# A third end slot of at most 32 rows, worked inside the last 256-row slot of a mixture-of-experts kernel

## The chip, the cores and the metric

The kernel runs on one core of a Trainium2 chip. The metric is the device time of one execution in microseconds, lower is better. Besides the times there is one profiled execution of the kernel before, whose trace is read below.

## The reference

A soft-capped attention feeds a layer of experts, of which every token goes to one:

```python
def _attn_ref(q, k, v, cap):                     # q, k, v: 8 x 12 x 448 x 64
    scores = cap * np.tanh(np.matmul(q, k.transpose(0, 1, 3, 2)) / np.sqrt(64) / cap)
    attn = softmax(scores)
    return np.matmul(attn, v)
...
x = attn_out.transpose(0, 2, 1, 3).reshape(3584, 768)
logits = x @ w_gate + modality_bias[modality_id]         # 8 experts
e_idx = np.argmax(logits, axis=1)
gate_w = softmax(logits)[np.arange(N), e_idx]
for e in range(8):
    mask = e_idx == e
    h = np.maximum(x[mask] @ w1[e], 0.0)                 # 768 x 1024
    out[mask] = gate_w[mask, None] * (h @ w2[e])         # 1024 x 768
```

With the reference's inputs the eight experts get 0, 245, 0, 1551, 0, 0, 0 and 1788 tokens.

## The kernel before, in words

**Attention and routing.** The first third of the run is attention in float32, in 64x64 tiles of TensorE. Each batch's rows of x are stored to DRAM, and a map is scattered there that has, region by region (one region for each expert), the token number, the gate weight and the softmax reciprocals of each row. `sums2` (L555) is the only place with 32-column tiles: four float32 products of 448 columns, each into its own 32 partitions of one PSUM bank, and four more behind them.

**Slots.** The experts' rows are worked in slots. A full slot has 384 rows (W, three tiles of 128). `slots` (L345) counts each expert's rows, gives it full slots as long as more than 256 rows are left, and sorts the remainders by size behind the full slots. Eight slots (one early one and seven, FIXED) are always run. What comes then depends on the data, and `slots` computes which of three endings fits: ENDS (L72) names their tiles, (2, 2, 1), (3, 2) and (3, 2, 1). `finish` (L1101) writes the endings as nested tests of one register. Only the body of the innermost one, ENDS[0], stands directly behind the tests:

```python
with tc.If(which == end + 1, preferred_fallthrough_block=end == 0) as branch:
```

ENDS[0] is three slots of 256, 256 and 128 rows; they are called A, B and C here.

**A slot** (`run_slot`, L1048). `gather` (L866) fetches the rows of the next slot from DRAM by an indirect DMA of POOL's queue. The weights of one expert are 6 raw blocks of W1 (512 KB each) and 8 of W2 (384 KB each). They are loaded on SP's queue into four staging buffers (`load_raw`, L888), and each is split into a rounded part (ScalarE, L899) and a remainder (VectorE, L900), so that three fast products take the place of one float32 product. `ffn1` (L934) makes 8 blocks of 128 hidden units, each over 6 blocks of the model dimension: for a slot of fewer than three tiles, two matmuls for each pair (L960, L961). Behind each block ScalarE and VectorE add the two halves (L968, L969), apply the rectifier (L972) and form the remainder (L973); in between stand the steps in `inside`: the last four W2 splits and the scaling of the next slot's rows (`norm`, L877). `ffn2` (L1000) makes, for each tile of 128 rows, two halves of 384 output columns, each from 24 matmuls (L1014), and between these halves the transposes of the next slot's rows (L916). ScalarE scales each half by the gate weight (L1030; the last half of all is cut between ScalarE and VectorE), and POOL scatters the tile to the output (L1043).

**Order of the work.** Engines take their instructions in order. An instruction that is pinned stays behind the one that was written before it on its engine; the others may be moved by the scheduler. SP's loads are pinned, and each waits for its staging buffer.

Of the kernel before, what the change touches and what calls it, by code (L numbers as in the profile page):

```python
# [52 lines left out]
NT, DM, FF, E, NM = B * S, H * D, 1024, 8, 2  # L53
# [7 lines left out]
TW = W // 128  # L61
RB = -(-NT // W)
RG = RB * W
NOROW = E * RG
ENTRY = 16
RECS = 4
HB = 32
# [1 line left out]
KC, FC = DM // 128, FF // 128  # L69
HALF = DM // 2  # L70
FIXED = 7
ENDS = ((2, 2, 1), (3, 2), (3, 2, 1))  # L72
MAXS = RB + E - 1
W2_EARLY = 4
LEAD = 3
# [10 lines left out]
class Program:  # L86
# [23 lines left out]
    def constants(self, cpool, dram):  # L110
        nc = self.nc
# [57 lines left out]
        self.blke = table("blke", [128, E, RB + 1], [[1, E], [0, RB + 1]])  # L169
        self.exp = table("exp", [128, E], [[1, E]])  # L170
        self.slot = table("slot", [128, 1], [[0, 1]], channel=1)

        self.acc = cpool.tile([CP, E], BF16, name="acc")
        nc.gpsimd.memset(self.acc, 0.0)
# [170 lines left out]
    def slots(self, pool, ps, early, then=None):  # L345
# [78 lines left out]
        if early:  # L424
            pair = tile("pair", [128, E])
            V.scalar_tensor_tensor(pair, rem, 128.0, sm, op0=ALU.is_gt, op1=ALU.mult)
            two = tile("two", [128, 1])
            V.tensor_reduce(two, pair, axis=AX.X, op=ALU.add)
            V.tensor_scalar(two, two, NB, float(FIXED + 2), op0=ALU.add, op1=ALU.is_le)
            first = tile("first1", [128, 1])  # L430
            V.scalar_tensor_tensor(first, NB, float(FIXED), two, op0=ALU.is_le, op1=ALU.mult)
            other = tile("other", [128, 1])
            V.scalar_tensor_tensor(other, NB, float(FIXED + 1), two, op0=ALU.is_le, op1=ALU.mult)
            V.tensor_tensor(other, other, first, op=ALU.subtract)
            V.tensor_scalar(begin, total, float(FIXED + 2), 2.0, op0=ALU.is_gt, op1=ALU.add)
            V.tensor_tensor(begin, begin, other, op=ALU.mult)
            V.tensor_tensor(end, begin, first, op=ALU.add)
            V.scalar_tensor_tensor(begin, first, 3.0, begin, op0=ALU.mult, op1=ALU.add)

            fits = tile("fits", [128, 1])  # L440
# [389 lines left out]
    def moe_pools2(self, st):  # L830
        pool = lambda name, bufs, **kw: st.enter_context(self.tc.tile_pool(name=name, bufs=bufs, **kw))
        wp = pool("wp2", 1)
        self.h = [wp.tile([128, FC, W], F32R, name=f"h{h}") for h in "hl"]
        self.w2s = [[wp.tile([128, DM], F32R, name=f"b{h}{k}") for h in "hl"] for k in range(W2_EARLY)]
        self.ps_h, self.ps_t, self.ps_y = (
            pool("ps_h", 3, space=PSUM), pool("ps_t", 2, space=PSUM), pool("ps_y", 2, space=PSUM)
        )
# [159 lines left out]
            finish(ph, f)  # L997
            hook("f", f)

    def ffn2(self, mt, n, between=(), wait=0, then=None, last=False):  # L1000

        nc = self.nc
        between = list(between)
        for t in range(n):
# [19 lines left out]
            for half in range(2):  # L1024
# [20 lines left out]
                bounds_check=NT - 1, oob_is_err=False,  # L1045
            )

    def run_slot(self, cur, n, ahead=None, raws=(), hooks=None, rows=None):  # L1048

# [23 lines left out]
        self.ffn2(cur[1], n, between=moves, wait=3 if hooks else 0, then=then if hooks else None, last=n < TW and not nxt)  # L1073
        return nxt

    def run_slots(self, cur, hooks):
# [24 lines left out]
    def finish(self, which, end, cur, ahead, rows):  # L1101

        tc = self.tc
        if end < 0:
            self.tail()
            return
        with tc.If(which == end + 1, preferred_fallthrough_block=end == 0) as branch:  # L1107
            at, self.last_sp = cur, None
            tiles = ENDS[end]
            for i, n in enumerate(tiles):  # L1110
                at = self.run_slot(
                    at, n, *((
                        lambda: ahead(FIXED + i + 1, tiles[i + 1]), (), None, lambda: rows(FIXED + i + 1, tiles[i + 1])
                    ) if i + 1 < len(tiles) else ())
                )
        with branch.Else():
            self.finish(which, end - 1, cur, ahead, rows)

# [119 lines left out]
    def build(self):  # L1238
        tc, nc = self.tc, self.nc
        with ExitStack() as st:  # L1240
# [3 lines left out]
            self.plani = self.cpool.tile([1, 3], I32, name="plani")  # L1244
            with ExitStack() as sa:
                qk = sa.enter_context(tc.tile_pool(name="qk", bufs=2))
                firsts = [qk.tile([128, FF], F32, name="kq") for _ in range(2)]
# [89 lines left out]
```

## Time and profile before

| | |
|---|---|
| median of 3 runs | 821.35 us (821.28 to 821.41) |
| the profiled execution, its own time | 819.97 us |
| its span, first to last instruction | 818.4 us |
| TensorE busy | 803.1 us, 98% of the span |
| VectorE, ScalarE, GpSimd busy | 518.5, 516.0, 139.2 us |
| moved by DMA | 148.44 MB, 181 GB/s over the span |

The busy time of an engine is the time in which it executed at least one instruction. Matmuls overlap, so a full TensorE row says that it had no gaps, not that it was at its peak. The time of one run lies some 1.6 us above the span of its profile, the median of the unprofiled runs 1.4 us above that run.

### The profile page before, as it was taken

To read this page: it belongs to the slowest core of one execution; us is meant where nothing else is said; L and a number is where in the kernel's file an instruction comes from. 1 tells how busy PE (TensorE), PEld (TensorE's weight loads), DVE (VectorE), ACT (ScalarE), POOL (GpSimd) and SP (SyncE) were. 2 spreads that over 40 slices of the span, in tenths; PEclk is the share of its full clock that TensorE was granted. 3 is DMA by queue.
4 is the path that set the end of the run, shared out by engine and by line. 5 is a ranking of instruction groups with operands and counts; after the bars stand their busy time and mean duration, and the time that the engine had idled before them with its cause. 6 is when DMAs were issued, how large, how long until landed. Compare 5 with 4: busy or idle time off the path is not lost. (4 is left out here: it accounts for less than half of the span.)

```text
span 818.4 us, 15444 instructions
## 1 busy us (share of the span) xinstructions
PE 803.1 (98%) x5988; PEld 608.9 (74%) x5988; DVE 518.5 (63%) x865; ACT 516.0 (63%) x655; POOL 139.2 (17%) x163
## 2 busy tenths in 40 slices
PE   7999999999999999999999999999999999999997
PEld 2333333333333348999999999999999999989996
DVE  4778888888788898764446344453544635447662
ACT  6999999999999994443444334444254443546562
POOL 2000220012021221451203113031120310111010
PEclk9999999999999999999999999999999999999999
DMA  5375536264454653977556365563665545557670
GB/s 187 116 218 194 144 131 203 74 200 147 149 181 137 189 188 89 274 233 277 208 178 230 117 216 209 189 204 135 205 230 186 200 151 183 167 190 254 219 222 29
DMA packets 57011, 148.44 MB, mean 181 GB/s; under 512 B 7758, under 2 KB 22366, under 8 KB 56928
## 3 DMA queue, kind: packets, MB, share of 16 engines
q1 hardware_dynamic: 48224, 113.34, 43.6%
q0 software_dynamic: 8560, 34.02, 11.6%
q8 instruction: 49, 0.80, 0.4%
q14 instruction: 34, 0.28, 0.1%
q10 hardware_dynamic: 144, 0.00, 0.0%
HBM read 114.44 MB, written 24.64 MB: 170 GB/s over the span
## 5 line engine op out<-in xcount | busy, mean ns | idle before, releaser
L961 PE MATMUL ph<-x,al 128*128 128x384 f32 (+2 forms) x510 | 159.9, 314 | 0.0
L1014 PE MATMUL py<-bh,hh 128*128 128x384 f32 x464 | 158.5, 342 | 0.4 <-ACT hh L972 0.3
L1014 PE MATMUL py<-bl,hh 128*128 128x384 f32 x464 | 155.6, 335 | 0.0
L1014 PE MATMUL py<-bh,hl 128*128 128x384 f32 x464 | 155.4, 335 | 0.0
L522 PE MATMUL xT<-pt,va 64*64 64x448 f32 x1344 | 151.8, 537 | 1.1 <-DVE xT L529 1.1
L494 ACT ACTIVATE pt<-sc 128x896 f32<-128x896 f32 x164 | 142.9, 906 | 11.4 <-PE sc L489 11.4
L497 ACT ACTIVATE pt<-pt 128x1792 f32<-128x1792 f32 x84 | 142.7, 1699 | 2.7
L510 DVE TENSOR_TENSOR tot<-tot,pt 128x896 f32<-128x896 f32 x118 | 127.7, 1082 | 10.8 <-ACT pt L497 6.4
L957 PE MATMUL ph<-x,ah 128*128 128x384 f32 x366 | 122.4, 334 | 0.0
L958 PE MATMUL ph<-x,ah 128*128 128x384 f32 x366 | 122.3, 334 | 0.0
L900 DVE TENSOR_TENSOR bl<-raw,bh 128x768 fp32r<-128x768 f32 x88 | 81.3, 954 | 52.6 <-ACT bh L899 52.6
L522 PEld LDWEIGHTS xT<-pt,va 64*64 64x64 f32 x1344 | 50.5, 133 | 73.7 <-issue 68.4
L1030 ACT ACTIVATE ot<-py,mt 128x384 f32<-128x384 f32 (+1 forms) x58 | 33.5, 579 | 102.6 <-PE py L1014 66.1
L972 ACT ACTIVATE hh<-ph 128x384 fp32r<-128x384 f32 x64 | 31.2, 491 | 105.7 <-PE ph L961 98.9
L961 PEld LDWEIGHTS ph<-x,al 128*128 128x128 f32 x510 | 96.0, 188 | 0.0
L900 DVE TENSOR_TENSOR al<-raw,ah 128x1024 fp32r<-128x1024 f32 x60 | 71.0, 1222 | 27.8 <-ACT ah L899 27.8
L1014 PEld LDWEIGHTS py<-bh,hh 128*128 128x128 f32 x464 | 87.1, 188 | 1.2 <-ACT hh L972 0.6
L1014 PEld LDWEIGHTS py<-bl,hh 128*128 128x128 f32 x464 | 87.2, 188 | 0.2 <-DVE bl L900 0.2
L1014 PEld LDWEIGHTS py<-bh,hl 128*128 128x128 f32 x464 | 87.1, 188 | 0.0
L899 ACT CAST bh<-raw 128x768 fp32r<-128x768 f32 x88 | 70.1, 836 | 24.2 <-DMA raw<-in_w_dram 24.0
L489 PE MATMUL sc<-kq 64*64 64x448 f32 x672 | 79.4, 547 | 3.7 <-ACT pt L494 2.6
L489 PE MATMUL sc<-kx 64*64 64x448 f32 x672 | 78.6, 540 | 0.8 <-ACT pt L494 0.8
(188 smaller groups left out, 909.6 us busy)
## 6 DMA issues: line engine op xcount, KB each, us to landing
raw<-in_w_dram SPq DMA_DIRECT2D x88, 384.0 KB, 4.5
raw<-in_w_dram SPq DMA_DIRECT2D x62, 512.0 KB, 4.1
kq<-in_kq_dram SPq DMA_DIRECT2D x24, 448.0 KB, 3.6
va<-in_v_dram SPq DMA_DIRECT2D x24, 448.0 KB, 5.5
kx<-in_kq_dram SPq DMA_DIRECT2D x24, 448.0 KB, 4.3
xd<-xs SPq DMA_DIRECT2D x32, 336.0 KB, 6.4
xr<-xg POOLq DMA_DIRECT2D x24, 384.0 KB, 3.1
mapd<-spare SPq DMA_DIRECT2D x4, 480.0 KB, 6.2
```

Source lines behind the costliest of these rows:

```text
L489: pin(pe.matmul(sc[i * KB : (i + 1) * KB, j, :S], kq[rows, s * KB : (s + 1) * KB], kq[rows, S:QK], start=True, stop=True,))
L494: pin(nc.scalar.activation(weights(n), sc[:, :, :S], AF.Tanh, scale=self.isc if slow else self.iscr))
L497: pin(nc.scalar.activation(pt, pt, AF.Exp, scale=self.cabsr))
L510: pin(V.tensor_tensor(tots[d], pt_of(n - 1) if s == 1 else tots[d], pt_of(n), op=ALU.add))
L522: pin(pe.matmul(self.xT[j * D : (j + 1) * D, i, :S], vas[d][rows, o : o + D], pt[rows, j], start=s == 0, stop=s == STEPS - 1,))
L899: keep((cast.tensor_copy if cast else self.nc.scalar.copy)(hi, raw))
L900: keep((minus or self.nc.vector).tensor_tensor(lo, raw, hi, op=ALU.subtract))
L957: keep(nc.tensor.matmul(ph[:, :w], hi[:, fs], self.x[:, k, 0, :w], start=first, stop=False))
L958: keep(nc.tensor.matmul(ph[:, :w], hi[:, fs], self.x[:, k, 1, :w], start=False, stop=False))
L961: keep(nc.tensor.matmul(ph[:, :w], lo[:, fs], self.x[:, k, 0, :w], start=False, stop=last))
L1014: nc.tensor.matmul(pys[half][:, :HALF], self.h[a][:, f, rows], self.w2s[f][c][:, cs], start=f == i == 0, stop=f == FC - 1 and i == 2,)
L1030: put = nc.scalar.mul(ot[:, half * HALF :][:, :cut], pys[half][:, :cut], mt[:, t, 1:2])
```

## The change

A fourth ending, (2, 2), is added. It is taken when the conditions of (2, 2, 1) hold and no more than two remainders have over 32 rows. The third remainder, of at most 32 rows, then has no slot of its own: its rows are gathered and scaled as 32 partitions, turned by six transposes (`few_turn`), and multiplied with the raw float32 weights, that are not split. The turned rows are the stationary operand (128 x 32) and the weights stream past them: a product over 128 of the model dimension is cut into four column groups of 32 columns, which write four 32-partition strips of one PSUM bank. So W1 takes 6 x 4 products of 256 columns (`few_first`), two transposes turn the hidden units (`few_back`), and W2 takes 8 x 4 products of 192 columns (`few_second`). The steps stand between the halves of slot B's `ffn2`. The fourteen raw blocks go to buffers that are free by then: the two first tiles of attention, a new tile `spare`, parts of the gathered rows' tile, and the four staging buffers.

```diff
-ENDS = ((2, 2, 1), (3, 2), (3, 2, 1))
+ENDS = ((2, 2, 1), (3, 2), (3, 2, 1), (2, 2))
+FEW = len(ENDS)
+FT = 32
+FG = 128 // FT
+FH, FY = FF // FG, DM // FG
...
+        for g in range(FG):
+            nc.gpsimd.memset(self.part[g * FT : (g + 1) * FT], float(g))
...
+            V.scalar_tensor_tensor(some, rem, float(FT), sm, op0=ALU.is_gt, op1=ALU.mult)
+            V.tensor_reduce(few, some, axis=AX.X, op=ALU.add)
+            V.tensor_scalar(few, few, NB, float(FIXED + 2), op0=ALU.add, op1=ALU.is_le)
+            V.tensor_tensor(few, few, first, op=ALU.mult)
+            V.scalar_tensor_tensor(end, few, float(FEW - 1), end, op0=ALU.mult, op1=ALU.add)
...
+        self.spare = wp.tile([128, DM], F32, name="w2f")
...
+                if 2 * t + half < len(besides):
+                    besides[2 * t + half]()
...
+    def few_rows(self):
+        few["e"] = self.register(nc.sync, meta[row : row + 1, 0:1], E - 1)
+        r = self.register(nc.gpsimd, meta[row : row + 1, 1:2], NOROW)
+        for g in range(FG):
+            self.pin(nc.gpsimd.dma_start(mt[g * FT : (g + 1) * FT], self.mapd[ds(r, FT)]))
+    def few_gather(self):
...
+    def few_ready(self):
+        self.pin(nc.vector.tensor_tensor(x, x, rec, op=ALU.mult))
+        self.pin(nc.vector.tensor_copy(spot, mt.bitcast(I32)[:, 0:1]))
+        self.pin(nc.vector.tensor_scalar(where, spot, float(FG), self.part, op0=ALU.mult, op1=ALU.add))
+        few["w1"] = [self.load_raw(few["e"], self.w1, k, FF, self.firsts[k]) for k in range(2)]
+        few["w2"] = [self.load_raw(few["e"], self.w2, 0, DM, self.spare)]
+    def few_weights(self):
+        few["w1"] += [self.load_raw(few["e"], self.w1, k, FF) for k in range(2, KC)]
+    def few_weights2(self):
+        dst = [self.xg[:, 2], self.xg[:, 0], self.firsts[0], self.firsts[1]] + [None] * 3
+        few["w2"] += [self.load_raw(few["e"], self.w2, f, DM, dst[f - 1]) for f in range(1, FC)]
+    def few_turn(self):
+        for k in range(KC):
+            self.pin(nc.tensor.transpose(
+                bank[:, k * FT : (k + 1) * FT], self.xg[:FT, 0, k * 128 : (k + 1) * 128], self.ident[:FT, :FT]
+            ))
+        self.pin(nc.scalar.copy(self.few["x"], ...))
+    def few_first(self):
+        for k in range(KC):
+            for g in range(FG):
+                self.pin(nc.tensor.matmul(
+                    bank[g * FT : (g + 1) * FT, :FH], few["x"][:, k], few["w1"][k][:, g * FH : (g + 1) * FH],
+                    start=k == 0, stop=k == KC - 1,
+                ))
+        self.pin(nc.scalar.activation(few["h"], bank[:, :FH], AF.Relu))
+        self.few_weights2()
+    def few_back(self):
+        for c in range(FH // 128):
+            self.pin(nc.tensor.transpose(bank[:, cs], few["h"][:, cs], self.ident))
+        self.pin(nc.scalar.copy(few["ht"], ...))
+    def few_second(self):
+        for f in range(FC):
+            for q in range(FG):
+                self.pin(nc.tensor.matmul(
+                    bank[q * FT : (q + 1) * FT, :FY], few["ht"][:, c, g * FT : (g + 1) * FT],
+                    few["w2"][f][:, q * FY : (q + 1) * FY], start=f == 0, stop=f == FC - 1,
+                ))
+        self.pin(nc.scalar.mul(ot[:, :FY], bank[:, :FY], few["mt"][:, 1:2]))
+        nc.gpsimd.indirect_dma_start(
...
     def run_slot(...):
+        if few:
+            inside += [self.few_ready, self.few_weights]
         self.ffn1(n, hooks, inside)
+        if few:
+            self.few_turn()
...
+                  besides=[self.few_first, self.few_back, self.few_second] if few else ())
...
     def finish(...):
+            tiles, few = ENDS[end], end + 1 == FEW
+            if few:
+                self.few_rows()
...
+                    at = self.run_slot(at, n, rows=self.few_gather if few else None, few=few)
```

## Rows read from the trace of the kernel before

**Rows 1.** Stretches: busy us of PE, PEld, DVE, ACT, POOL; clock, DMA share, GB/s.

```profile
758.86:775.51 16.65, 16.65 (x98) 14.68 (x97) 11.32 (x21) 8.65 (x19) 1.58 (x2) 1.00 0.80 264
775.51:792.78 17.27, 17.27 (x104) 17.16 (x103) 11.70 (x17) 12.13 (x21) 1.37 (x1) 1.00 0.58 180
792.78:803.83 11.05, 11.05 (x97) 11.05 (x97) 7.71 (x19) 6.80 (x19) 0.99 (x1) 1.00 0.53 172
803.83:812.41 8.58, 8.54 (x50) 8.22 (x49) 0.88 (x3) 1.26 (x4) 0.00 (x0) 1.00 0.01 2
812.41:818.40 5.99, 0.00 (x0) 0.00 (x0) 0.42 (x1) 0.42 (x1) 0.98 (x1) 0.72 0.07 19
```

**Rows 2.** DMA issues and queues, 805 to 818.4: name, count, us to landing; packets, MB.

```profile
out_dram<-ot,mt POOLq DMA_INDIRECT x1, 3.1
...
q0 software_dynamic: 80, 0.05, 1.5%
```

**Rows 3.** Timeline of TensorE in slots B and C: start us, us, instruction.

```profile
775.51 0.34 PE L1014 MATMUL py<-bh,hh 128*128 128x384 f32 x1
...
779.68 0.29 PE L916 MATMUL ptr<-identr,xr 128*128 128x128 f32 x2
779.80 0.41 PE L1014 MATMUL py<-bh,hh 128*128 128x384 f32 x1
...
792.78 0.28 PE L960 MATMUL ph<-x,ah 128*128 128x256 f32 x1
...
812.03 0.34 PE L1014 MATMUL py<-bh,hl 128*128 128x384 f32 x1
```

**Rows 4.** Timeline of TensorE in attention, around one call of `sums2`.

```profile
36.60 0.96 PE L561 MATMUL glog<-tot,pick 128*32 128x448 f32 x8
37.38 0.94 PE L563 MATMUL glog<-xT,wgt 128*32 128x448 f32 x8
38.24 0.61 PE L489 MATMUL sc<-kq 64*64 64x448 f32 x4
```

**Rows 5.** Timeline of TensorE: six transposes between two halves of `ffn2`.

```profile
700.81 0.63 PE L916 MATMUL ptr<-identr,xr 128*128 128x128 f32 x6
```

**Rows 6.** POOL's map loads (ns), gather of slot B's rows, its landing (us), its scaling.

```profile
L860 POOL DMA_DIRECT2D mt<-mapd x6: 537/557/606, 344.5 to 348.9; - x6
...
727.01 1.40 POOL L869 DMA_INDIRECT xg<-xd,mt  x1 [0.30 <-issue]
...
xg<-xd,mt POOLq DMA_INDIRECT x2, 7.1
...
739.77 0.95 DVE L881 TENSOR_TENSOR xg<-xg,mt 128x768 f32<-128x768 f32 x1
```

**Rows 7.** Timeline of VectorE: one of the planner's small operations.

```profile
331.32 0.15 DVE L437 TENSOR_TENSOR plan<-plan,first 128x1 f32<-128x1 f32 x1
```

**Rows 8.** Waits of TensorE over the run: line, waited for, us in total, times, longest.

```profile
PE ptr L916 <- DVE xg L881: 0.6, 1, 0.6
```

**Rows 9.** The scatter that starts at 724.3: its landing.

```profile
L1043 POOL DMA_INDIRECT out_dram<-ot,mt x1: 985/985/985, 724.3 to 724.3; - x1
...
DMA to landing us min/median/max: 3.1/3.1/3.1
```

**Rows 10.** Sequencers at the end tests and behind: ns min/median/max, first and last start.

```profile
L1107 PEldq COMPARE_BRANCH  x4: 63/66/3289, 720.6 to 809.3; - x4
L1107 ACTq COMPARE_BRANCH  x4: 34/34/38, 723.5 to 812.5; - x4
...
L1332 ACTq DRAIN  x2: 8/44/80, 815.4 to 817.8; - x2
```

**Rows 11.** Timeline of TensorE and ScalarE behind the end tests, slot A.

```profile
723.29 0.39 PE L960 MATMUL ph<-x,ah 128*128 128x512 f32 x1
...
735.27 0.50 PE L960 MATMUL ph<-x,ah 128*128 128x512 f32 x1 [0.87 <-DVE acc L969]
...
723.97 0.83 ACT L899 CAST bh<-raw 128x768 fp32r<-128x768 f32 x1
```

More of the change, by code (lines that the diff above doesn't have):

```diff
@@ L171, in constants @@
         self.slot = table("slot", [128, 1], [[0, 1]], channel=1)
+        self.part = cpool.tile([128, 1], F32, name="part")
+        for g in range(FG):
+            nc.gpsimd.memset(self.part[g * FT : (g + 1) * FT], float(g))
         self.acc = cpool.tile([CP, E], BF16, name="acc")
@@ L998, in ffn1, with ffn2 @@
             hook("f", f)
-    def ffn2(self, mt, n, between=(), wait=0, then=None, last=False):
+    def ffn2(self, mt, n, between=(), wait=0, then=None, last=False, besides=()):
         nc = self.nc
@@ L1046, in ffn2 @@
             )
-    def run_slot(self, cur, n, ahead=None, raws=(), hooks=None, rows=None):
+    def few_rows(self):
+        nc, meta, row = self.nc, self.meta, FIXED + 2
+        few = self.few = {}
+        few["e"] = self.register(nc.sync, meta[row : row + 1, 0:1], E - 1)
+        r = self.register(nc.gpsimd, meta[row : row + 1, 1:2], NOROW)
+        mt = few["mt"] = self.mp.tile([128, ENTRY], F32, name="mf", bufs=1)
+        for g in range(FG):
+            self.pin(nc.gpsimd.dma_start(mt[g * FT : (g + 1) * FT], self.mapd[ds(r, FT)]))
@@ new lines, in few_weights, with few_bank @@
+    def few_weights(self):
+        few = self.few
+        few["w1"] += [self.load_raw(few["e"], self.w1, k, FF) for k in range(2, KC)]
+    def few_weights2(self):
+        few = self.few
+        dst = [self.xg[:, 2], self.xg[:, 0], self.firsts[0], self.firsts[1]] + [None] * 3
+        few["w2"] += [self.load_raw(few["e"], self.w2, f, DM, dst[f - 1]) for f in range(1, FC)]
+    def few_bank(self):
+        return self.ps_r.tile([128, 512], F32, name="few", tag="small")
+    def few_turn(self):
+        nc = self.nc
+        bank = self.few_bank()
+        for k in range(KC):
+            self.pin(nc.tensor.transpose(
+                bank[:, k * FT : (k + 1) * FT], self.xg[:FT, 0, k * 128 : (k + 1) * 128], self.ident[:FT, :FT]
+            ))
+        self.pin(nc.scalar.copy(self.few["x"], bank[:, : KC * FT].rearrange("p (k t) -> p k t", k=KC)))
@@ new lines, in few_second @@
+    def few_second(self):
+        nc, few = self.nc, self.few
+        bank = self.few_bank()
+        for f in range(FC):
+            g, c = divmod(f, FH // 128)
+            for q in range(FG):
+                self.pin(nc.tensor.matmul(
+                    bank[q * FT : (q + 1) * FT, :FY], few["ht"][:, c, g * FT : (g + 1) * FT],
+                    few["w2"][f][:, q * FY : (q + 1) * FY], start=f == 0, stop=f == FC - 1,
+                ))
+        ot = self.op.tile([128, DM], F32, name="ot")
+        self.pin(nc.scalar.mul(ot[:, :FY], bank[:, :FY], few["mt"][:, 1:2]))
+        nc.gpsimd.indirect_dma_start(
+            self.out.rearrange("n (q c) -> (n q) c", q=FG),
+            bass.IndirectOffsetOnAxis(ap=few["at"][:, 0:1], axis=0), ot[:, :FY], None,
+            bounds_check=FG * NT - 1, oob_is_err=False,
+        )
@@ L1054, in run_slot @@
+    def run_slot(self, cur, n, ahead=None, raws=(), hooks=None, rows=None, few=False):
         moves, inside = [], []
@@ L1072, in run_slot @@
             moves = [lambda k=k: self.transpose(k, *pool(k), n=nxt[2], raw=bool(hooks)) for k in range(KC)]
-        self.ffn2(cur[1], n, between=moves, wait=3 if hooks else 0, then=then if hooks else None, last=n < TW and not nxt)
+        self.ffn2(cur[1], n, between=moves, wait=3 if hooks else 0, then=then if hooks else None, last=n < TW and not nxt,
+                  besides=[self.few_first, self.few_back, self.few_second] if few else ())
         return nxt
@@ L1108, in finish @@
             at, self.last_sp = cur, None
-            tiles = ENDS[end]
+            tiles, few = ENDS[end], end + 1 == FEW
+            if few:
+                self.few_rows()
             for i, n in enumerate(tiles):
[L1111 to L1115, printed above, removed]
+                if i + 1 < len(tiles):
+                    at = self.run_slot(
+                        at, n, lambda: ahead(FIXED + i + 1, tiles[i + 1]), rows=lambda: rows(FIXED + i + 1, tiles[i + 1])
+                    )
+                else:
+                    at = self.run_slot(at, n, rows=self.few_gather if few else None, few=few)
         with branch.Else():
@@ L1246, in build @@
                 qk = sa.enter_context(tc.tile_pool(name="qk", bufs=2))
-                firsts = [qk.tile([128, FF], F32, name="kq") for _ in range(2)]
+                firsts = self.firsts = [qk.tile([128, FF], F32, name="kq") for _ in range(2)]
                 for g, first in enumerate(firsts):
```

21 lines of the change are left out of this document (added).

## The prediction

> **What bounds the kernel now.** I read the busy time by stretch first, for the last three slots' ends [rows 1]: TensorE is busy for the whole of each stretch (16.65 of 16.65 us, 17.27 of 17.27, 11.05 of 11.05, 8.54 of 8.58), at the full granted clock (1.00), while VectorE and ScalarE have a third of each stretch free and the DMA share falls from 0.80 to 0.01. So what TensorE no longer does is time, as long as nothing takes its place; behind its last matmul stands a tail of 5.99 us without TensorE. Then the DMA rows of the last microseconds [rows 2], which show how full slot C is: its scatter moves 0.05 MB, some 16 rows of 768 float32. That agrees with the counts of the inputs, 1551 - 4 x 384 = 15 rows; the other remainders are 252 and 245. TensorE works 128 columns for 15 rows there. Last the timelines, for prices.
>
> **What is removed.** Slot C: its first matmul starts at 792.78, its last at 812.03 [rows 3]. Matmuls of this kind follow each other at (779.68 - 775.51) / 24 = 0.174 us [rows 3], so C holds TensorE for 812.03 + 0.17 - 792.78 = 19.4 us. The transposes of C's rows between slot B's halves go too: two of them take 0.12 us, and the matmul behind them is 0.07 us longer than others (0.41 against 0.34) [rows 3]; three such places give 0.6 us. Together 20.0 us. The splits of C's fourteen weight blocks on ScalarE and VectorE go as well, which had no time on the path. The fourteen loads stay.
>
> **What is added on TensorE.** All of it goes between B's halves, and TensorE has no free time there, so all of it counts.
> - The 24 + 32 raw float32 products. The nearest row is `sums2` [rows 4]: four products of 448 columns into four column groups, eight instructions in the trace, take 37.38 - 36.60 = 0.78 us, or 0.195 us a product, 0.435 ns a column. `few_first` is 24 x 256 columns, `few_second` 32 x 192 columns: 2.67 us each. Bounds: below, these 5.3 us (nothing makes a column cheaper than there); above, 0.195 us for each product whatever its columns, 10.9 us. I take the lower end, since the form (128 x 32, float32, four groups) is the same and 256 columns are over half of 448.
> - Six transposes of 32 rows: six of 128 rows took 0.63 us [rows 5]; I take 0.63. Two more in `few_back`: 0.21 us.
> - Going into and out of another tile form, eight times. Behind the second four products of `sums2` the next form starts after 38.24 - 37.38 = 0.86 us in place of 0.78 [rows 4]: 0.08 us each, 0.64 us; between nothing and twice that.
>
> A rule speaks against this last price. The Trainium skill, TensorEngine Tiling (Array Packing), Key Properties, says that a change of the tiling mode drains TensorE. Taken as the part of a matmul that normally overlaps the next (0.34 - 0.17 us, [rows 3]) it would be an estimated 1.4 us for eight changes in place of 0.64; the trace shows the smaller figure.
>
> Sum added: 2.67 + 2.67 + 0.63 + 0.21 + 0.64 = 6.8 us. Left: 20.0 - 6.8 = 13.2 us gained.
>
> **What lies beside other work.**
> - The fourteen loads. From 759 to `few_first` SP has to bring two more blocks for B's W2, six of W1 and two of W2, 4.7 MB. At the 264 GB/s of that stretch [rows 1] this takes 17.9 us, to 777; `few_first` starts at 775.51 + 0.8 + 24 x 0.174 = 780.5. Cover: 3.6 us. The last five W2 blocks (2.0 MB) wait for `few_first` to free their buffers; at 180 GB/s [rows 1] they are there by 781 + 11 = 792, when `few_second` starts (780.5 + 2.8 + 4.2 + 0.4 + 4.2 = 792.1) and goes through them in order. I cost both at nothing.
> - POOL, at the end tests: one register load and four map loads at 0.557 us [rows 6], 2.2 us and a little, ahead of the gathers of B's rows. The second gather starts at 727.01 and lands 7.1 us behind its issue [rows 6], at 734; some 2.5 us later it is 736.6, and its scaling stands at 739.77 [rows 6]. 3 us of cover: nothing. Without it VectorE's in-order queue, B's transposes and TensorE would wait.
> - ScalarE's four added steps and VectorE's three (the scaling replaces C's) have the time of the splits that are gone: nothing. Four memsets at the start stand beside the wait for the first loads: nothing.
> - Five operations in the planner, 0.15 us each [rows 7]. TensorE waits 0.6 us once for scaled rows of the slot behind the planner [rows 8], so this may be on the path: between 0 and 0.75 us, I take 0.3.
> - The tail: the last scatter now carries a tile of 117 valid rows. A full tile's scatter with idle DMA, the one at 724.3, landed in 3.1 us [rows 9], as did C's almost empty one [rows 2]. Nothing. The small scatter goes out 4.2 us before, longer than such a landing.
>
> **The jump.** The three tests now fall through in 34 to 66 ns [rows 10], since ENDS[0] stands behind them. The new body doesn't, so every engine must jump to it. The only jumps in the trace are those at the body's end: TensorE's sequencer was held 3.29 us there, and ScalarE's next instruction comes 815.4 - 812.5 = 2.9 us behind its own [rows 10]. At the tests TensorE's sequencer is ahead by 723.29 - 720.6 = 2.7 us [rows 10, 11], so a stall of 3.3 us shows 0.6 us, and slot A has 0.87 us of idle time on another chain [rows 11]. Between 0 and 0.6, I take 0.3. ScalarE's part is a rival.
>
> **The number.** 13.2 - 0.3 - 0.3 = 12.6 us. The profiled execution (819.97 us, span 818.4) would be 807.4; the median of the runs lies 1.4 us above it: 821.35 - 12.6 = **808.8 us**. By the drain of the Trainium skill's TensorEngine Tiling (Array Packing), Key Properties, it would be an estimated 809.5.
>
> **Rivals.**
> - **ScalarE's jump shows (0.20).** ScalarE reaches the tests only at 723.5 and starts A's splits at 723.97 [rows 10, 11], without a queue ahead of it. If its jump costs the 2.9 us of the one at the end, the splits start at 726.4, 2.4 us late, SP's next loads wait for their buffers, and the wait of TensorE for `acc` at 735.27 grows by as much. Against it: the new body lies only ENDS[0]'s length behind the tests, the end jump goes past all endings. 808.8 + 2.4 - 0.3 = 810.9. The Trainium skill, Runtime: NRT & Kernel Launch, Instruction fetch mechanics, says that a taken branch whose target is outside the window of two fetched pages stalls for its fetch; the end jumps agree, and whether this target is inside no run here shows.
> - **Short passes are not cheaper (0.12).** If each product costs 0.195 us whatever its columns, 56 cost 10.9 us and not 5.3: 814.4.
> - **Weights late (0.06).** If the loads before `few_first` run at the 180 GB/s of the next stretch [rows 1], 4.7 MB take 26.2 us, to 785.2: 4.7 us of stall, 813.5.
> - **The column groups run one behind the other (0.03): slower.** Then the products cost four times 5.3 us, 21.4 us, and the time is 808.8 + 16 = 824.8. It turns at 5.3 + 12.6 = 17.9 us, that is when fewer than 1.2 of four groups run at once. `sums2` speaks against it: eight instructions of 448 columns end within 0.96 us, 0.12 us each, though one of 384 columns lasts 0.34 us [rows 3, 4]. For it speaks only that there the four streams came from different tiles.
> - **The ending is not chosen (0.02).** With remainders 252, 245 and 15 the condition (seven full slots and two remainders above 32 make nine) holds, and the 0.05 MB [rows 2] agree. Otherwise 821.4.
>
> **How the numbers follow.** The forecast's own case has 0.57; its bounds (switches free or doubled, the small transposes at half their price, jump and planner at their ends) give 807.2 to 810.2. The range goes on to 813.6, which takes in the ScalarE jump and the late weights and leaves out the short passes at their full price, the slower case and the ending not chosen. A change of less than 0.2%, 1.6 us, could not be told from none. Faster than that are the forecast and the first three rivals, 0.95; the same 0.02; slower 0.03.
>
> **What would show it.** TensorE's timeline should end its last half near 799.5, with four uninterrupted halves of 4.2 us; `few_first` and `few_second` should each take 2.7 to 3 us, without waits for weights; the splits of A should start at 724, not 726.4; the tail should stay at 6 us. The prediction is wrong if the products take over 4 us each, if TensorE shows waits for raw weights, or if the start of slot A has a gap of over 1 us.

## The result and the profile after

The changed kernel takes 808.93 us (median of 4 runs, 808.17 to 812.46) against 821.34 (821.28 to 821.41) for the kernel before beside it. The ratio of the means is 0.9857, with a 95% interval of 0.9828 to 0.9886: 11.7 us less, between 9.4 and 14.1. The medians differ by 12.4 us; the run at 812.46 makes the difference between the two. The forecast was 808.8, 12.6 us less. The profiled execution took 809.34 us, its span is 807.7.

The page of the changed kernel, busy time by engine (us, share of the span, instructions): TensorE is still the bound, and now has 98% of a shorter span.

```profile
PE 791.6 (98%) x5958; PEld 594.2 (74%) x5958; DVE 501.1 (62%) x836; ACT 500.4 (62%) x621; POOL 140.6 (17%) x170
```

To see where the time went, the scatters serve as marks, since POOL issues one behind every finished tile. The timeline of POOL in the kernel before: the last scatters of the second and the eighth full slot, of slot A and of slot C.

```profile
414.59 0.98 POOL L1043 DMA_INDIRECT out_dram<-ot,mt  x1 [7.87 <-ACT ot L1030]
...
724.35 0.98 POOL L1043 DMA_INDIRECT out_dram<-ot,mt  x1 [7.86 <-ACT ot L1030]
...
759.92 0.99 POOL L1043 DMA_INDIRECT out_dram<-ot,mt  x1 [7.91 <-ACT ot L1030]
...
813.56 0.98 POOL L1043 DMA_INDIRECT out_dram<-ot,mt  x1 [18.73 <-POOLq L1107]
```

The same marks in the changed kernel (the last line is slot B's last tile):

```profile
415.91 0.98 POOL L1061 DMA_INDIRECT out_dram<-ot,mt  x1 [7.93 <-ACT ot L1046]
...
726.36 0.98 POOL L1061 DMA_INDIRECT out_dram<-ot,mt  x1 [7.93 <-ACT ot L1046]
...
761.95 1.00 POOL L1061 DMA_INDIRECT out_dram<-ot,mt  x1 [7.98 <-ACT ot L1046]
...
802.39 0.98 POOL L1061 DMA_INDIRECT out_dram<-ot,mt  x1 [3.82 <-POOLq L1229]
```

They cut the span into five stretches: up to the second slot's last scatter; the six full slots behind it; slot A; from A's last scatter to the start of the last matmul (slots B and C, or B with the few rows in it); and the tail. Worked out so for all fourteen profiled executions of this study, in us (the experiments are told below; the lower eight ran in other sets, in which the kernel before took 828 to 831 us; the unaltered changed kernel takes about 8 us longer there too, nearly all of it in the first stretch; the span is known to 0.1 us, so the tail is good to 0.05):

| execution | to slot 2 | six slots | A | B (and C) | tail |
|---|---|---|---|---|---|
| before | 414.59 | 309.76 | 35.57 | 52.11 | 6.37 |
| e_before_tile | 415.57 | 309.76 | 35.21 | 52.10 | 6.26 |
| after | 415.91 | 310.45 | 35.59 | 38.91 | 6.84 |
| after_again | 415.75 | 310.20 | 36.13 | 38.88 | 6.94 |
| e_spare_last | 413.94 | 310.20 | 35.68 | 38.88 | 6.90 |
| e_fall | 415.10 | 310.20 | **34.66** | 38.88 | 6.96 |
| e_group_order | 424.11 | 310.20 | 36.07 | **44.13** | 6.89 |
| e_half_columns | 424.05 | 310.20 | 35.83 | 38.91 | 6.91 |
| e_maps3 | 422.89 | 310.45 | **40.95** | 38.90 | 6.81 |
| e_first_early | 424.28 | 310.45 | 35.80 | 38.94 | 6.93 |
| after_beside | 422.94 | 310.20 | 36.39 | 38.91 | 6.86 |
| e_align | 424.53 | **309.69** | 35.38 | 38.84 | 6.86 |
| e_tail_rows | 423.27 | 310.20 | 36.13 | 38.88 | **6.32** |
| e_best | 425.47 | 311.69 | 35.10 | 39.00 | 7.14 |

Whole runs of one program spread by one to four microseconds; the stretch of B repeats within 0.1 us. Against the two programs without the change, the three executions of the change in the upper sets that jump to its body (after, after_again, e_spare_last) have on average +0.1 in the first stretch, +0.5 in the six slots, +0.4 in A, -13.2 in B and C, +0.6 in the tail: 11.6 us in all, near the ratio's 11.7 and 0.8 short of the medians' 12.4. The first stretch, which differs by 2 us between executions of one program, is enough to hide that much.

TensorE's timeline in slot B, changed kernel, around the four added steps (L1119 turns the rows, L1130 is `few_first`, L1143 turns the hidden units, L1153 is `few_second`; L1030 is `ffn2`, which was L1014):

```profile
777.41 0.28 PE L977 MATMUL ph<-x,al 128*128 128x256 f32 x1
777.62 0.56 PE L1119 MATMUL few<-ident,xg 32*128 32x32 f32 x6
...
778.39 0.34 PE L1030 MATMUL py<-bl,hh 128*128 128x384 f32 x1
...
782.24 0.34 PE L1030 MATMUL py<-bh,hl 128*128 128x384 f32 x1
782.51 1.07 PE L1130 MATMUL few<-kq,xg 128*32 128x256 f32 x16
783.40 1.91 PE L1130 MATMUL few<-raw,xg 128*32 128x256 f32 x32
785.24 0.44 PE L1030 MATMUL py<-bh,hh 128*128 128x384 f32 x1
785.52 0.34 PE L1030 MATMUL py<-bl,hh 128*128 128x384 f32 x1
...
789.35 0.34 PE L1030 MATMUL py<-bh,hl 128*128 128x384 f32 x1
789.52 0.38 PE L1143 MATMUL few<-ident,xg 128*128 128x128 f32 x2
...
789.92 0.34 PE L1030 MATMUL py<-bl,hh 128*128 128x384 f32 x1
...
793.75 0.34 PE L1030 MATMUL py<-bh,hl 128*128 128x384 f32 x1
794.02 0.53 PE L1153 MATMUL few<-w2f,xg 128*32 128x192 f32 x8
...
797.03 0.34 PE L1030 MATMUL py<-bl,hh 128*128 128x384 f32 x1
```

No row of this stretch has an idle time in brackets: TensorE waits neither for raw weights nor for a copy. The cost of a step, switches included, is the way from the last matmul ahead of it to the second behind it, less the 0.17 us that each of the two takes at the normal pace [rows 3]: turn 778.39 - 0.17 - 777.53 = 0.69 (the matmul ahead of it, shorter, would have been followed after 0.12), `few_first` 785.35 - 782.41 = 2.94, back 789.75 - 789.52 = 0.23, `few_second` 796.86 - 793.92 = 2.94. Together 6.80 us, where the prediction had 6.8.

The branch at the end tests, changed kernel, by sequencer (ns min/median/max, first and last start; of two each, the first is the test):

```profile
L1229 SPq COMPARE_BRANCH  x2: 38/48/58, 703.0 to 785.9; - x2
L1229 DVEq COMPARE_BRANCH  x2: 53/63/73, 722.4 to 801.8; - x2
L1229 PEldq COMPARE_BRANCH  x2: 3460/3524/3589, 722.6 to 798.1; - x2
L1229 ACTq COMPARE_BRANCH  x2: 38/44/50, 725.5 to 801.3; - x2
L1229 POOLq COMPARE_BRANCH  x2: 47/52/58, 726.5 to 802.2; - x2
```

And from the view of TensorE's waits the only one behind the tests (line, waited for, us in total, times, longest):

```profile
PE ph L976 <- issue: 0.8, 1, 0.8
```

The jump holds TensorE's sequencer longest, for 3.5 us, of which 0.8 us shows (0.6 to 1.0 in the ten executions that jump). For the other four the length of the branch itself says little, because the 2.9 us that the prediction read for ScalarE at the body's end [rows 10] lie behind a branch of 38 ns, on the way to the next instruction. Measured so at the test, that way is 0.2 us on POOL, 0.5 on ScalarE and SP and 0.6 on VectorE, by the start times in the trace, where it is 0.1 us or less in e_fall (below), which doesn't jump. ScalarE's first split shows what is left of it:

```profile
726.05 3.04 ACT L915 CAST bh<-raw 128x768 fp32r<-128x768 f32 x4
```

It starts 0.54 us behind the scaling ahead of it (725.51), where it was 0.48 before (723.49 to 723.97), so 0.06 us of ScalarE's jump shows. The wait for `acc` within A [rows 11] is gone.

The last scatter's landing in the changed kernel, in the view of its line, is 3.7 us; the one in [rows 2] took 3.1. The two single lines at the end are SP's waits for semaphores that stand behind this landing at the program's end, of the changed kernel and of the one before: eleven in 0.75 us, and eight in 0.56.

```profile
L1061 POOL DMA_INDIRECT out_dram<-ot,mt x1: 980/980/980, 802.4 to 802.4; - x1
...
DMA to landing us min/median/max: 3.7/3.7/3.7
```

```profile
L1457 SPq EVENT_SEMAPHORE  x11: 27/28/28, 806.2 to 806.8; - x11
```

```profile
L1332 SPq EVENT_SEMAPHORE  x8: 28/28/28, 816.7 to 817.1; - x8
```

### The profile page after: what moved, and what is told of

The parts are those of the page before. It is cut to its first block, busy times and chain, and to the rows that moved or that the text cites. A ratio compares the mean times of both kernels' runs of the same rounds, so it can differ in the third digit from the quotient of the medians.

```text
span 807.7 us, 15307 instructions
## 1 busy us (share of the span) xinstructions
PE 791.6 (98%) x5958; PEld 594.2 (74%) x5958; DVE 501.1 (62%) x836; ACT 500.4 (62%) x621; POOL 140.6 (17%) x170
## 5 line engine op out<-in xcount | busy, mean ns | idle before, releaser
L1030 PE MATMUL py<-bh,hh 128*128 128x384 f32 x448 | 153.8, 344 | 0.4 <-ACT hh L988 0.3
L1030 PE MATMUL py<-bl,hh 128*128 128x384 f32 x448 | 150.8, 337 | 0.0
L1030 PE MATMUL py<-bh,hl 128*128 128x384 f32 x448 | 150.4, 336 | 0.0
L509 ACT ACTIVATE pt<-sc 128x896 f32<-128x896 f32 x164 | 142.9, 906 | 11.8 <-PE sc L504 11.7
L977 PE MATMUL ph<-x,al 128*128 128x384 f32 (+1 forms) x462 | 149.1, 323 | 0.0
L916 DVE TENSOR_TENSOR bl<-raw,bh 128x768 fp32r<-128x768 f32 x80 | 74.0, 955 | 49.4 <-ACT bh L915 49.0
L977 PEld LDWEIGHTS ph<-x,al 128*128 128x128 f32 x462 | 86.8, 188 | 0.0
L1030 PEld LDWEIGHTS py<-bh,hh 128*128 128x128 f32 x448 | 84.0, 188 | 1.9 <-issue 0.7
L1030 PEld LDWEIGHTS py<-bl,hh 128*128 128x128 f32 x448 | 84.1, 188 | 0.2 <-DVE bl L916 0.2
L1030 PEld LDWEIGHTS py<-bh,hl 128*128 128x128 f32 x448 | 84.1, 188 | 0.0
L916 DVE TENSOR_TENSOR al<-raw,ah 128x1024 fp32r<-128x1024 f32 x54 | 63.9, 1222 | 24.1 <-ACT ah L915 24.0
L318 POOL DMA_INDIRECT mapd<-pay,pos x32 | 34.8, 1087 | 252.4 <-DVE pos L311 206.2
```

What stands on the lines that cost most here:

```text
L318: put = nc.gpsimd.indirect_dma_start(self.mapd, bass.IndirectOffsetOnAxis(ap=pos[:, c : c + 1], axis=0), pay[:, c, :], None, bounds_check= ...
L509: pin(nc.scalar.activation(weights(n), sc[:, :, :S], AF.Tanh, scale=self.isc if slow else self.iscr))
L916: keep((minus or self.nc.vector).tensor_tensor(lo, raw, hi, op=ALU.subtract))
L977: keep(nc.tensor.matmul(ph[:, :w], lo[:, fs], self.x[:, k, 0, :w], start=False, stop=last))
L1030: nc.tensor.matmul(pys[half][:, :HALF], self.h[a][:, f, rows], self.w2s[f][c][:, cs], start=f == i == 0, stop=f == FC - 1 and i == 2,)
```

## The experiments

The theory after the result: the change gains 13.2 us in B and C as worked out; a jump, a longer last scatter and a slower pace in the full slots give back some 1.5 us. Each part had a rival.

**The same kernel again.**

> The changed kernel once more, unaltered. In its first four runs it took 808.17, 808.52, 809.34 and 812.46 us, the kernel before 821.28 to 821.41. Theory A: the 812.46 is a rare accident; the median comes to 808.2 to 809.0 with at most one run above 810. Theory B: the change brings a spread of its own (some stretch that starts early or late by chance), and again about one run in four lies 2 us or more above the rest.

808.27 to 809.44 us in four runs, median 808.9, ratio 0.9851 (0.9835 to 0.9867); theory A. The kernel before, though, spread from 819.66 to 822.81 in 15 runs of this set, so the 0.13 us of its first four runs had understated its spread. None of these 15 lies more than 1.5 us above the median, and 812.46 lay 3.5 above; it did not come back, and its cause is not known.

**No jump.**

```diff
-with tc.If(which == end + 1, preferred_fallthrough_block=end == 0) as branch:
+with tc.If(which == end + 1, preferred_fallthrough_block=end in (0, FEW - 1)) as branch:
```

> The test for the new ending made to fall through, so that no engine jumps to its body. Theory A: the jump's 3.5 us on TensorE's sequencer is hidden but for the 0.8 us that TensorE stands idle at the start of slot A, and that idle time takes the place of the 0.87 us wait for acc at 735.27 which was there before; without the jump this wait comes back and the time changes by under 0.3 us. Theory B: the 0.8 us is time on the path of its own; the kernel gets 0.8 us faster. Theory C (ScalarE's jump costs the prediction's 2.4 us unseen): over 2 us faster.

The whole run doesn't tell (808.48 against 808.9 us, both spread by more). The stretch does: slot A takes 34.66 us, where nine executions with the jump take 35.38 to 36.39 (e_maps3, with its added wait, stands aside). POOL's timeline of e_fall:

```profile
725.30 0.99 POOL L1061 DMA_INDIRECT out_dram<-ot,mt  x1 [7.90 <-ACT ot L1046]
...
759.96 0.99 POOL L1061 DMA_INDIRECT out_dram<-ot,mt  x1 [7.78 <-ACT ot L1046]
```

From 725 to the end the view of TensorE's waits has no row at all: neither the issue gap nor the wait for `acc`. Theory B: the gap goes and no wait comes in its place. The stretch is 0.7 to 1.7 us shorter, 1.2 against the average of 35.9; the gap itself is 0.6 to 1.0 us, so a part of the difference stands in no wait of the trace. It rests on one execution: e_best, the only other one without the jump, takes 35.10, with a slower pace of its matmuls and a wait of 0.2 us. Against the kernel before the change loses less than that, because the 34.66 is also 0.6 to 0.9 us below the stretch of before, which had the wait for `acc` in it (0.9 us in the one execution, 0.3 in e_before_tile). Theory C falls.

**The addresses of the halves of W2, first try.**

```diff
+        self.w2s = [[wp.tile([128, DM], F32R, name=f"b{h}{k}") for h in "hl"] for k in range(W2_EARLY)]
         self.spare = wp.tile([128, DM], F32, name="w2f")
-        self.w2s = [[wp.tile([128, DM], F32R, name=f"b{h}{k}") for h in "hl"] for k in range(W2_EARLY)]
```

(`h`, too, is ahead of `spare` now.)

> The new 3 KB buffer for the first raw W2 block allocated behind the halves of h and W2 and not ahead of them, so that these lie at the addresses they had before the change. In the profile of the changed kernel each ffn2 (144 matmuls) takes 0.10 to 0.16 us longer than before, 0.7 to 0.9 us over seven slots. Theory A: that is the shifted addresses; the matmuls of ffn2 get back to their former spacing and the kernel is 0.7 to 0.9 us faster. Theory B: it is something else that differs between two executions or programs; no change beyond 0.2 us.

Theory B: the six slots still take 310.20 us, and the run 808.92 in the median.

**The same shift in the kernel before.**

```diff
+        self.spare = wp.tile([128, DM], F32, name="w2f")
         self.h = [wp.tile([128, FC, W], F32R, name=f"h{h}") for h in "hl"]
```

> The kernel before with one unused 3 KB tile ahead of h and the halves of W2, which shifts their addresses as the change does, and nothing else. Theory A (addresses): each ffn2 gets 0.10 to 0.16 us longer, 0.8 to 1.2 us over the eight full slots and the ends: 822.2 to 822.5 us. Theory B: no change, 821.35 within 0.2 us.

Theory B: 820.99 us, ratio 0.9997 (0.9988 to 1.0006), six slots in 309.76. A shift by 3072 bytes does nothing to them.

**The order of the column groups.**

```diff
-        for k in range(KC):
-            for g in range(FG):
+        for g in range(FG):
+            for k in range(KC):
```

> few_first's 24 products go out column group after column group (six products into one group, then six into the next) in place of going round the four groups. Same products, same columns. Theory A (products in different column groups run at the same time only where they are neighbours in TensorE's stream): few_first takes four times its 2.73 us, about 10.9 us, and the stretch from slot A's last scatter to the last matmul 47.0 us in place of 38.9: 816 to 818 us. Theory B (a product costs its 0.11 us whatever its neighbours are): few_first stays at 2.7 us and the stretch at 38.9 us.

B takes 44.13 us, 5.25 more than 38.88. That is theory A with another size. The timeline of TensorE: the first group from its start to where the second sets in, and the matmul behind the step. (A product is two instructions; `kq` holds the weights of a group's first two products, `raw` those of its last four.)

```profile
790.91 1.05 PE L1130 MATMUL few<-kq,xg 128*32 128x256 f32 x4
791.80 1.24 PE L1130 MATMUL few<-raw,xg 128*32 128x256 f32 x5
792.67 0.40 PE L1130 MATMUL few<-kq,xg 128*32 128x256 f32 x1
792.88 0.38 PE L1130 MATMUL few<-raw,xg 128*32 128x256 f32 x1
792.91 0.38 PE L1130 MATMUL few<-kq,xg 128*32 128x256 f32 x1
...
798.89 0.44 PE L1030 MATMUL py<-bh,hh 128*128 128x384 f32 x1
```

The step takes 798.89 - 790.91 = 7.98 us, 0.33 a product, where going round the four groups it takes 2.73, 0.114 a product. So going round four groups gives a factor of 2.9 over staying in one, and all of it hangs on the order. The rows also show why it is not four. Four instructions of one group take 791.80 - 790.91 = 0.89 us here, and sixteen instructions of four groups take as long in the changed kernel (782.51 to 783.40): a group's own pace is the same, and the order sets how many groups run at once. Where two groups meet, the second starts (792.67) while the first still has three instructions to start, and from there on the two run side by side (792.88 and 792.91). The forecast's price per column, read from `sums2`, held because `few_first` goes round the groups as `sums2` does [rows 4]. The Trainium skill, TensorEngine Tiling (Array Packing), Key Properties, says that tiles work independently and can execute in parallel; the run agrees, for tiles that are next to each other in the stream.

**The price of a product.**

```diff
-        for g in range(FG):
+        for c in range(2):
+            for g in range(FG):
 ...
-            bank[g * FT : (g + 1) * FT, :FH]
+            bank[g * FT : (g + 1) * FT, c * 128 : (c + 1) * 128]
```

> Each of few_first's 24 products of 256 columns is issued as two of 128 columns: 48 products, the same columns in all. Theory A (the price is 0.435 ns a column in four groups, with nothing per product): few_first stays at 2.7 us, the stretch from slot A's last scatter to the last matmul at 38.9 us within 0.2. Theory B (the price is per product, 0.11 us): few_first takes 5.4 us, the stretch 41.6 us. Between the two, the price would have a fixed part.

Theory A: B takes 38.91 us, and the 48 products the time of the 24 (TensorE's timeline; start us, us):

```profile
790.61 1.08 PE L1132 MATMUL few<-kq,xg 128*32 128x128 f32 x32
791.51 1.93 PE L1132 MATMUL few<-raw,xg 128*32 128x128 f32 x64
793.37 0.44 PE L1030 MATMUL py<-bh,hh 128*128 128x384 f32 x1
```

790.61 to 793.37 is 2.76 us; it was 782.51 to 785.24, 2.73. Going round four groups, there is no fixed price of a product down to 128 columns, so the rival of short passes falls.

**POOL's cover.**

```diff
-        for g in range(FG):
+        for g in 3 * list(range(FG)):
             self.pin(nc.gpsimd.dma_start(mt[g * FT : (g + 1) * FT], self.mapd[ds(r, FT)]))
```

> few_rows loads its four map blocks three times in a row: POOL issues eight loads more (0.557 us each, 4.5 us) ahead of the gathers of B's rows. The prediction gave the four loads 3 us of cover, of which they use 2.2. Theory A (that cover is all there is): the normalisation of B's rows comes 3 to 4 us later, behind it in VectorE's queue the accumulations of slot A, and TensorE stands for 1 to 4 us within slot A. Theory B (the gathers land long before they are wanted, since POOL waited 7.7 us for the transfer of the scaled rows anyway): under 0.3 us.

A takes 40.95 us, 5.1 more than the 35.9 of the others, beyond theory A's most, and on another way than it had. The loads into the same tile waited for each other's landing, and the scheduler put four of the eight ahead of the second gather and four behind it. That gather was 3 us late (741.97 - 733.34 = 8.6 us behind the eighth slot's last scatter, where it is 5.6 in the changed kernel), and VectorE's scaling waited 1.9 us for it. More was lost on POOL: the transfers of the scaled rows went out at 753.25 only, behind a wait of 6.5 us that the trace puts down to a product of TensorE; what held them there was not tried. TensorE's waits, and then its busy time by stretch (the columns are those of [rows 1]):

```profile
PE ptr L932 <- DMA xr<-xg: 3.3, 2, 1.8
```

```profile
758.00:760.00 2.00, 1.98 (x11) 1.98 (x12) 1.02 (x4) 1.59 (x3) 0.00 (x0) 0.83 1.01 405
760.00:762.00 2.00, 2.00 (x8) 2.00 (x7) 1.19 (x1) 0.00 (x0) 0.00 (x0) 0.50 0.90 333
762.00:764.00 2.00, 2.00 (x11) 2.00 (x11) 0.00 (x0) 0.00 (x0) 0.00 (x0) 0.81 0.71 201
764.00:766.00 2.00, 2.00 (x15) 1.97 (x14) 0.13 (x1) 1.69 (x4) 0.82 (x1) 1.00 0.00 0
```

TensorE's wait shows at the transposes of B's rows, not inside `ffn1`, as 3.3 us in two pieces. Behind it the granted clock goes from 1.00 to 0.50 (from 2.4 to 1.2 GHz) and is back at 764: eight matmuls in two microseconds where there are fifteen at the full clock. Twelve matmuls from 759.25 on take 3.65 us, where at 0.174 they would take 2.09: that is 1.6 of the 1.8 us by which the stretch grew beyond the wait. Theory B falls: the cover on POOL is finite, and running out of it costs half as much again as the wait. In the changed kernel itself it doesn't run out.

**`few_first` earlier.**

```diff
         if few:
             self.few_turn()
+            self.few_first()
 ...
-besides=[self.few_first, self.few_back, self.few_second]
+besides=[lambda: None, self.few_back, self.few_second]
```

> few_first goes directly behind few_turn, 4.4 us earlier, in place of behind the first half. Theory A (the raw W1 blocks are there at 777, as the prediction had it): no wait for weights; TensorE waits some 0.6 us for ScalarE's copy of the turned rows, two switches of the tile form fall away (0.08 us each): 0.3 to 0.6 us slower, the stretch from slot A's last scatter to the last matmul 39.2 to 39.5 us. Theory B (the weights only just come): up to 4.4 us slower, with waits of TensorE for the raw blocks.

B takes 38.94 us, no slower. The expected wait for ScalarE's copy didn't come because the scheduler put eight matmuls of the first half in between (TensorE's timeline):

```profile
786.20 0.56 PE L1119 MATMUL few<-ident,xg 32*128 32x32 f32 x6
786.69 0.44 PE L1030 MATMUL py<-bh,hh 128*128 128x384 f32 x1
...
788.31 1.07 PE L1130 MATMUL few<-kq,xg 128*32 128x256 f32 x16
```

So `few_first` moved by some 2.8 us and not 4.4, measured from the turning of the rows, and no switch fell away. It still met all its weights: they have at least that much to spare. Theory B falls.

**The unaltered kernel beside the last three.**

> The changed kernel unaltered, as the neighbour of the next three on the same chip. Ratio to the kernel before 0.983 to 0.987. The six slots between two last scatters (slots 2 to 7 of the seven full ones) take 310.20 or 310.45 us, as in all seven programs so far that hold the change, against 309.76 in both that don't; slot A with its jump 35.6 to 36.1 us; from A's last scatter to the last matmul 38.9 us; from the last matmul's start to the end of the span 6.8 to 6.95 us.

817.19 us against 830.47, ratio 0.985 (0.9829 to 0.987); the stretches came as expected but for A's 36.39, in which TensorE waited 0.5 us for a turned block besides.

**The addresses, second try.**

```diff
+        cpool.tile([128, 1], F32, name="pad")
         self.part = cpool.tile([128, 1], F32, name="part")
```

> One more four-byte constant, which takes 32 bytes of each partition and moves everything behind it (x, the halves of W1, h, the first four of W2) by 32 bytes: they start again at 32 past a multiple of 64, as in the kernel before, and no longer at a multiple of 64. The 3 KB buffer had shifted by a multiple of 64, which is why moving it changed nothing. Theory A (the alignment sets the pace of ffn2's matmuls): the six full slots take 309.76 us again, 0.44 to 0.69 us less. Theory B (something else in the program): 310.20 or 310.45 us.

The six slots took 309.69 us: theory A, in this execution. A group of TensorE's costliest over the six slots (busy us and mean ns behind the first bar), first of after_beside, then of e_align:

```profile
L1030 PE MATMUL py<-bh,hh 128*128 128x384 f32 x288 | 98.7, 343 | 0.0
```

```profile
L1031 PE MATMUL py<-bh,hh 128*128 128x384 f32 x288 | 98.5, 342 | 0.0
```

It is a nanosecond a matmul, here and in the two other groups. In the whole run, 817.43 against 817.19 us, it can't be seen.

**The size of the last scatter.**

```diff
+            some = FT if last and t == n - 1 else 128
             nc.gpsimd.indirect_dma_start(
-                self.out, bass.IndirectOffsetOnAxis(ap=mt.bitcast(I32)[:, t, 0:1], axis=0), ot, None,
+                self.out, bass.IndirectOffsetOnAxis(ap=mt.bitcast(I32)[:some, t, 0:1], axis=0), ot[:some], None,
```

> The last scatter sends only the first 32 of the 128 rows of its tile; the others, valid rows among them, are left out of the output. The tail from the last matmul's start to the end is 6.8 to 6.95 us with the change and was 6.3 to 6.4 before, when the last scatter had 15 valid rows. Theory A (the landing of 117 valid rows takes 0.55 us longer than that of 15): the tail is 6.3 to 6.4 us again. Theory B (the end itself is longer with the change, the last branch or the small scatter ahead): it stays at 6.8 to 6.95 us.

Theory A: the tail is 6.32 us again, 0.5 less than beside it, while the last branch and the small scatter are as before. The last scatter's queue moves 0.10 MB in 32 packets and no longer 0.36 MB in 80 (the DMA queues of the tail, first of the changed kernel, then of this one):

```profile
q0 software_dynamic: 80, 0.36, 23.5%
```

```profile
q0 software_dynamic: 32, 0.10, 8.9%
```

So fewer rows in the last transfer shorten the end; whether by their number or by their bytes, this run doesn't tell. The tail's growth is not the landing alone. By the records of the sequencers SP's list of waits ends last in the changed kernel, while in the two kernels with a short landing (this one and the one before) POOL ends 0.3 to 0.4 us behind that list. From the kernel before to the changed one the landing grew by 0.66 us, three more waits behind it took 0.19, and 0.31 had been hidden behind POOL: 0.54 in all.

**All three together.** The fallthrough of e_fall, the 32 bytes of e_align, and the last tile in two scatters of 384 columns:

```diff
+                if last and besides and t == n - 1:
+                    nc.gpsimd.indirect_dma_start(
+                        self.out.rearrange("n (q c) -> (n q) c", q=2),
+                        bass.IndirectOffsetOnAxis(ap=at2[:, half : half + 1], axis=0),
+                        ot[:, half * HALF :][:, :HALF], None, bounds_check=2 * NT - 1, oob_is_err=False,
+                    )
```

> Three things in one: the test for the new ending falls through, the 32 bytes of e_align, and the last tile's two column halves are scattered one by one, the first when it is ready (its rows of 384 columns each), so that the last scatter moves half the bytes in as many rows. Theory A for each: slot A in 34.6 to 34.9 us (no jump), the six slots in 309.76 us, the tail 6.55 to 6.65 us if the bytes set its longer landing; in all 1.5 to 2 us faster than the changed kernel. Theory B: the tail stays at 6.85 us or over if the number of rows sets it; the six slots stay at 310.2 if alignment doesn't matter; then only slot A's 1 us is gained.

A miss: 818.14 us, no faster than the 817.19 of the changed kernel. A took 35.10 us, without the issue gap. The tail grew to 7.14 us, for a reason that no theory had. POOL's timeline and its waits:

```profile
805.58 0.98 POOL L1063 DMA_INDIRECT out_dram<-ot,at  x1 [3.69 <-ACT ot L1053]
810.22 0.98 POOL L1173 DMA_INDIRECT out_dram<-ot,at  x1 [3.66 <-DMA out_dram<-ot,at]
813.24 0.98 POOL L1063 DMA_INDIRECT out_dram<-ot,at  x1 [2.04 <-POOLq L1243]
```

The small scatter at 810.22 waited for the landing of the half scatter ahead of it. The last then starts 813.24 - 811.26 = 1.98 us behind the last matmul's start, where it was 1.53, and 2 us behind POOL's previous instruction. By the records of POOL's sequencer it waited for the small scatter's landing in turn: that wait ends at 812.49 and the scatter starts 0.75 us later, as the small one had started 0.75 behind the end of its own wait (809.47). Why three scatters to separate rows wait for each other was not tried; all three write the output through rearranged views. From the last one's start to the end of the span are 5.2 us against 5.3 beside it: half the bytes in as many rows give 0.1 to 0.2 us, and the wait takes 0.45. The six slots took 311.69 us although the 32 bytes are in as in e_align; the profiled execution was also the slowest of its four (820.02 us, the others 817.12 to 818.17).

## Why the prediction was right

- **Removed 20.0, added 6.8 in B and C: right.** Slots B and C gave 52.1 - 38.9 = 13.2 us, as worked out (13.2). The added steps measure 6.80: the two product steps 2.94 each against 2.83 with their switches, the transposes 0.92 against 1.16. The lower bound taken for the products, so much per column, is confirmed by e_half_columns, and what it needs by e_group_order. With 6.80 added and 13.2 gained, the 20.0 removed are confirmed too.
- **Switches of the tile form: right.** Ahead of `few_first` the way is 0.27 in place of 0.17, behind it 0.28: 0.1 us each. By the drain of the Trainium skill's TensorEngine Tiling (Array Packing), Key Properties, as it was priced there, B would have gained 12.4 us and not 13.2; if the switch drains the engine, as it says, that is all it costs here.
- **Weights, POOL, ScalarE, VectorE at nothing: right** in the changed kernel, and for the first two with the limits tested: some 2.8 us to spare for the weights of `few_first`; on POOL less than the three-fold map loads take.
- **The jump at 0.3: right within its bounds.** Slot A came out 0.4 us longer on the average (0.0 to 0.9 between single executions). But two parts make it up: TensorE's sequencer was held 3.5 us in place of 3.3, and 0.8 of it showed in place of at most 0.6; and the wait for `acc` left in turn, which the prediction named but did not subtract. Against the same program without a jump the price is larger, 0.7 to 1.7 us by the one execution of e_fall.
- **ScalarE's jump (rival, 0.20): wrong.** Its next instruction came 0.5 us behind the test and not 2.9, and its splits 0.06 us later. The Trainium skill, Runtime: NRT & Kernel Launch, Instruction fetch mechanics, says that a taken branch whose target is outside the two fetched pages stalls for its fetch. The rows agree as far as they go: TensorE, which has by far the most instructions, was held 3.5 us and the four others 0.1 to 0.5. No run here moved a target across a page.
- **The planner at 0.3:** not seen. The first stretch is 0.1 us longer on the average, between executions that differ by two.
- **The tail at nothing: the one step that failed.** It measured 0.6 us. The step took one landing, 3.1 us at 724.3 [rows 9], for that of every full tile. The last one lands in 3.7 us, and e_tail_rows shows that the tail is as short as before when that scatter sends fewer rows. At the end the landing is followed by SP's list of waits, which no term of the prediction had; as it fell out, three more of them stand behind the landing than before.
- **What the prediction didn't have:** 0.5 us in the six full slots, of which nothing is changed in the source.

So the stretches give 13.2 - 0.4 - 0.1 - 0.6 - 0.5 = 11.6 us, the forecast 12.6, the medians 12.4. The mechanism was right; that the median fell within 0.2 us of the forecast is luck, because terms of 0.5 and 0.6 us were left out and 1 us is less than these runs spread.

## What to carry to other kernels

On this path, which TensorE bounds, a tile of 128 rows with 15 valid ones cost 20 us; streaming raw float32 weights past a 32-column stationary operand, going round the four column groups, did the same 15 rows for 6.8 us. Issue the groups in turn, not one after the other. When work is removed from the end, look at what the last transfer carries afterwards, and measure small parts by stretches between marks of the trace: whole runs hid each of the half-microsecond effects here.

## What was not expected

- **The pace of `ffn2`.** Seven executions of the changed program and its variants took 310.20 us for the six slots, three 310.45, both programs without the change 309.76, and e_align, whose operands again start at 32 past a multiple of 64 bytes, 309.69. That speaks for the alignment, with one execution; e_best, with the same 32 bytes and 311.69, shows that something else moves the pace too. It stays open.
- **A wait's second price.** Behind 3.3 us of waiting for rows TensorE's granted clock went to 0.50, and 1.8 us more were lost.
- **A full tile's landing has no one value.** The scatter behind the eighth slot, 3.1 us in the kernel before [rows 9], took 3.8 in the changed one and 3.1 again in e_fall; the last one, with no load beside it, took 3.7 to 3.8 in the four executions of a whole tile whose trace has it. So a tile's size alone doesn't set it. Why some take 3.1 was not tried.
